# The same 1,706 steps in another order: the last 1,144 places of a written-out list, DeltaNet and a multiplicative FFN in one kernel

## The chip, the cores and the metric

One core of a Trainium2 chip runs the whole program. The metric is the device time of one execution in microseconds (us). TensorE is PE in the profile (its weight loads are PEld), VectorE is DVE, ScalarE is ACT, GpSimd is POOL, and SyncE is SP, which here issues all DMAs.

## The reference

A DeltaNet attention block over `q, k, v` of (4 batches, 8 heads, 768 tokens, 48) and `beta`, then a feed-forward block over its 3,072 tokens of 384 features, all float32.

```python
k_n = k / (norm(k) + 1e-6)
for t in range(S):
    y[t]  = q[t] @ state                       # state: 48 x 48 per batch and head
    v_old = state^T k_n[t]
    state = state + beta[t] * outer(k_n[t], v[t] - v_old)
x = y as (3072, 384)
out = ((x @ w1) * (x @ w2)) @ w3 @ w_out       # w1, w2: 384 x 1024; w3: 1024 x 1024; w_out: 1024 x 384
```

## The kernel before, in words

The recurrence is cut into 12 chunks of 64 tokens, two chunks to a pair (u = 0 to 5). Inside a chunk the recurrence is a triangular system. The kernel inverts its 32 x 32 blocks on DVE, and the rest is small matmuls on TensorE. The feed-forward part runs on the 512 tokens of a pair with w3 @ w_out folded into one weight (w34, 1024 x 384) at the start. From u = 1 on, the two products with w1 and w2 are made by a scheme with sums of operands that saves matmuls, and the product with w34 is made by a Strassen-like scheme for all u.

Each part is a Python generator. One `next` of it is a **step** and issues the instructions of one engine (a group of matmuls, one elementwise operation, a few DMAs). A string, `ORDER`, lists which part takes its next step. So the n-th mention of a name is always that part's step n (counted from 0), wherever it stands. After the list has been walked, `in_text_order` ties every instruction to the one before it on its engine: **each engine runs its own instructions in the list's order**, SP its DMAs too. Between engines only data and buffers set the order.

```python
    def step(name):
        other[:] = name[len(name.rstrip("'")):]     # a prime: the other engine
        ...
        next(running[name], None)

    for name in ORDER.split():
        step(name)
    in_text_order()
```

The names, with the lines of the profile:
- `p m` (L297), 2 steps: SP loads the keys (8 DMAs), then the queries of chunk m, from m = 4 on into the same buffer. `d m` (L390), 4: DVE transposes the two halves of the keys, then of the queries. `k`, `v` (L269, L280): SP loads more copies of keys and values.
- `s m` (L456, L462), twice: PE makes the scores, DVE scales a part (L468), ACT copies the rest (L480), POOL masks it (L482).
- `u m` (L522): SP writes blocks of the scores to DRAM. `V j`, for the two chunks of a pair: 0 loads them back (L533), 1 and 2 set up a PSUM buffer on ACT, **3 to 33 are 31 pairs of dependent DVE operations** (L564, L569), 34 and 35 copy out on ACT (L578), 36 writes to DRAM. From step 1 to 36 V holds one of the two large PSUM buffers (`ps_w`); the products of s, e, c and y then share the other one.
- `e m`: 0 loads the inverse's blocks on SP (L594, L601), 1 transposes on DVE (L622), 2 and 4 are PE products (L639), 3 and 5 are ACT's reads of them (L664, L684).
- `c m`: 0, 2 and 4 are PE products (L710), 1, 3 and 5 DVE's reads of them (L741: residual, L750: X, L772: the next state). Each product needs the read before it, product 2 also e's result.
- `y m` (L809): PE makes a chunk's outputs, ACT copies them (L828), SP completes them for a pair (L839).
- `n`, `g`, `N`: normalizers of the values and keys, on POOL, DVE and ACT.
- `G u`: POOL's sums of token blocks (L200). `m u0`, `m u1`: 47 steps each, in which PE adds a product into one of four PSUM banks (`ps_f`, L1140, two matmuls of 256 columns) and ACT (L1164, L1168) or DVE (L1166, L1171) reads it; step 30 (29 in `m u0`), 36 (34), 45 (44) and 46 multiply two results elementwise (L200).
- `S u`: POOL's sums of those results (L200), eight steps for u > 0. `oA u` to `oD u`: eight matmuls of 192 columns a step (L1222), A, B and C with two steps. `xA u` to `xD u`: ACT and DVE read those banks (L1252, L1257, L1259), SP stores the result (L1239). Banks come free for m of the next pair only by these reads. The last pair has `o5` and `x5`.
- `a`, `b` (L938): the two plain products of u = 0. `W`, `T`: POOL's sums of weights.

G, S, W and the elementwise products run on POOL; with a prime behind the name (`S4'`) on DVE:

```python
    def alone(out, x, y, op):
        (dve if other else pool).tensor_tensor(out=out, in0=x, in1=y, op=op)
```

PSUM banks and most buffers are handed out in turn at the step that first uses them (`in_turn`), so a list in another order also hands them out in another order.

Of the kernel before, what the change touches and what calls it, by code (L numbers as in the profile page):

```python
# [70 lines left out]
s6 G2 G2 m20 m20 m20 m20 m20 V3 m20 m20 m20 g4 V3 V3 V3 xC1 m20 m20 m20 d8 m20 m20 m20 m20 V3 V3 m20
d8 N3 m20 m20 m20 m20 m20 m20 m20 m20 m20' c6 m20 m20 m20 m20 m20 m21 g4 V3 e6 e6 m20 e6 m20 m20 m21
m21 e6 e6 m20 m20 g4 g4 m20 m20 g4 m21 m21 m21 e6 c6 c6 s8 m21 m21 m21 m21 N4 N4 s8 s8 m21 y6 m21
m21 m21 y6 c6 s8 p9 e7 e7 d9 d9 m21 m21 m21 m21 m21 m21 m21 c6 s8 e7 m21 s8 m21 m21 m21 p9 m21 e7 s8
d9 d9 m21 m21 m21 m21 m21' m21 s9 s9 s9 k10 s7 g5 s9 s9 n7 m21 m21 m21 s9 m21 m21' m21 m21 u8 e7 s9
c7 m21 m21 m21 c7 m21 u9 V4 S2' m21 m21 oA2 e7 m21' m21 S2 S2 g5 V4 S2 xA2 c7 oD2 V4 V4 V4 V4 c7 y7
V4 V4 V4 V4 V4 V4 p10 d10 V4 V4 y7 oB2 oA2 S2 s8 S2 S2 xB2 v8 y7 S2 d10 V4 V4 V4 V4 xA2 xA2 oB2 oC2
xB2 xD2 V4 V4 xC2 V4 V4 V4 V4 V4 V4 xC2 G3 G3 G3 m30 V4 m30 m30 xD2 m30 oC2 xC2 G3 G3 m30 m30 G3 G3
G3 G3 G3 m30 c7 m30 V4 V4 V4 V4 V4 m30 m30 m30 m30 m30 m30 m30 m30 m30 m30 m30 m30 V4 g5 n8 V4 V4 V4
v9 p10 k11 xC2 m30 m30 m30 G3' G3 m30 m30 m30 m30 m30 m30 m30 m30 m30 m30 m30 m30 c7 V4 e8 m30 m30  # L80
d10 m30 m30 m30 m30 m31 m30 m30 m31 m31 e8 e8 m30 e8 m31 c8 m31 e8 e9 g5 g5 n8 m30 m30 m31 m31 g5 g5
d10 g5 e8 n9 m30 n9 e9 c8 e9 c8 N4 m31 m31 m31 m31 m31 e9 m31 N5 m31 c8 y8 y8 N5 m31 m31 m31 p11 d11
# [13 lines left out]
m50 m50 m50 m50 m50 m51 m50 m50 m50 m50 m51 m51 m51 m51 m50 m50 m51 m50' m51 m51 m51 m51 m51 m51 m51
m51 m51 m51 m51 m51 m51 m51 m51 m51 m51 m51 m51 m51 m51 m51 m51 m51 m51 m51 m51 m51 m51 m51 S5' m51
m51 m51 m51 m51 m51 m51 m51 m51 m51 S5' o5 S5 m51' x5 S5 o5 o5 o5 o5 S5' S5 o5 x5 S5' x5 x5 S5' o5
x5 x5 x5 x5 x5 x5 x5 x5 x5 x5
# [1331 lines left out]
```

## Time and profile before

| | us |
|---|---|
| time, median of 3 runs (lowest, highest) | 545.23 (544.31, 548.61) |
| time of the profiled execution | 541.36 |
| its span, from the first to the last instruction | 539.7 |
| PE busy in it | 513.8 |
| DVE busy | 401.4 |
| POOL busy | 274.1 |
| ACT busy | 220.4 |

The profile names a wait by the engine that waits, its line, and what ended the wait. In the timeline the first number is the start in us from the span's start, the second the length, and `[0.85 <-DVE KQ L390]` says that the engine stood idle for 0.85 us until DVE's write of KQ at L390. A matmul in float32 is two instructions in the trace, so `x4` at L1140 is one step of m. The ends of matmuls are modelled; their starts are not, and times of steps are taken from start to start.

### The profile page before, as it was taken

The page shows a single profiled execution, that of the slowest core. Times are in us where ns is not written, and L with a number is a line of the kernel's source. Part 1 is how long each engine was busy: PE and PEld are TensorE (multiplying, and loading weights), DVE is VectorE, ACT ScalarE, POOL GpSimd, SP SyncE. Part 2 cuts the span into 40 slices and gives each one's busy share as a digit, 9 for nine tenths or more (in the row PEclk, how much of TensorE's full clock was granted, in tenths as well). Part 3 has the DMA queues.
Part 4 walks back from the last instruction along what each step waited for, and adds up shares of the span by engine and source line. Part 5 has one row for each costly group of instructions (what it writes and reads, how often), then busy time and mean ns, then how long its engine had stood idle before and what let it go on. Part 6 is the DMA issues. An engine that isn't in the chain of part 4 may idle for free.

```text
span 539.7 us, 19914 instructions
## 1 busy us (share of the span) xinstructions
PE 513.8 (95%) x8466; PEld 431.7 (80%) x8466; DVE 401.4 (74%) x880; ACT 220.4 (41%) x453; POOL 274.1 (51%) x296
## 2 busy tenths in 40 slices
PE   6779988999999999999999999999999999999997
PEld 3645557688888987789888889878799788997886
DVE  2789966898668997868997799887779855536562
ACT  3697567747534034432034433245321352312210
POOL 4585664244889996067832258361378402051150
PEclk8599998999999999999999999999999999999999
DMA  9969964869653354654454561733314220010001
GB/s 223 315 155 237 220 107 121 159 154 152 95 86 70 74 128 69 98 118 75 92 105 61 82 119 46 146 70 50 57 51 109 75 41 4 17 56 3 2 1 58
DMA packets 195544, 52.64 MB, mean 98 GB/s; under 512 B 182528, under 2 KB 189824, under 8 KB 195456
## 3 DMA queue, kind: packets, MB, share of 16 engines
q1 hardware_dynamic: 195456, 51.38, 46.3%
q8 instruction: 66, 1.08, 0.8%
q14 instruction: 22, 0.18, 0.1%
HBM read 41.25 MB, written 8.91 MB: 93 GB/s over the span
## 4 chain that ended last, share of the span: by engine, by line
PE 77%; DVE 6%; SPq 6%; DMA 4%; issue 3%; ACT 2%; POOL 1%; DVEq 0%; ACTq 0%; POOLq 0%
PE ps_f L1140 27%; PE ps_f L1222 20%; PE ps_f L938 8%; PE ps_w L710 6%; PE ps_f L918 5%; PE ps_w L809 4%; SPq L297 3%; PE ps_w L639 2%; PE ps_w L456 2%; PE ps_w L462 1%; DMA X<-in_q_dram 1%; DMA TT<-Vd 1%; SPq L269 1%; DVE KQ L390 1%; DMA perm<-in_q_dram 1%
## 5 line engine op out<-in xcount | busy, mean ns | idle before, releaser
L200 POOL TENSOR_TENSOR ab<-ab 128x512 f32<-128x512 f32 (+1 forms) x57 | 65.5, 1168 | 67.3 <-DVE ab L1171 33.7
L1222 PE MATMUL ps_f<-w,ab 128*128 128x192 f32 x376 | 65.1, 327 | 0.0
L1140 PE MATMUL ps_f<-xT,w1s 128*128 128x256 f32 x240 | 63.5, 388 | 0.1
L1140 PE MATMUL ps_f<-xT,w2s 128*128 128x256 f32 x240 | 61.6, 387 | 1.0 <-DVE x_room L1171 1.0
L1222 PEld LDWEIGHTS ps_f<-w,ab 128*128 128x128 f32 x376 | 61.9, 190 | 0.6
L1171 DVE TENSOR_TENSOR ab<-ab,ps_f 128x512 f32<-128x512 f32 x70 | 47.6, 683 | 16.7 <-PE ps_f L1140 15.0
L1140 PEld LDWEIGHTS ps_f<-xT,w1s 128*128 128x128 f32 x240 | 43.5, 189 | 9.8 <-ACT x_room L1168 2.0
L1140 PEld LDWEIGHTS ps_f<-xT,w2s 128*128 128x128 f32 x240 | 43.7, 189 | 8.6 <-DVE x_room L1171 1.5
L482 POOL TENSOR_TENSOR PT<-PT,smask 128x512 f32<-128x512 f32 x20 | 25.4, 1273 | 46.0 <-ACT PT L480 45.9
L1222 PE MATMUL ps_f<-room,ab 128*128 128x192 f32 x272 | 47.2, 329 | 0.8 <-DVE room L1252 0.8
L569 DVE TENSOR_TENSOR ps_w<-ps_w,tb 128x31 f32<-128x31 f32 (+15 forms) x124 | 43.3, 349 | 4.5
L564 DVE TENSOR_TENSOR tb<-ps_w,Ub 128x31 f32<-128x31 f32 (+15 forms) x124 | 41.9, 338 | 5.2 <-DMA Ub<-Ud 2.1
L918 PE MATMUL ps_f<-w2s,w3T 128*128 128x384 f32 x128 | 43.8, 492 | 1.7 <-POOL w2s L867 1.1
L1222 PEld LDWEIGHTS ps_f<-room,ab 128*128 128x128 f32 x272 | 44.2, 190 | 1.4 <-POOL xT L200 0.9
L828 ACT COPY xT<-ps_w 48x256 f32<-48x256 f32 x96 | 30.5, 365 | 33.6 <-PE ps_w L809 33.1
L200 POOL TENSOR_TENSOR xT<-xT 128x256 f32<-128x256 f32 x44 | 31.8, 738 | 21.0 <-DVE xT L200 15.2
L1140 PE MATMUL ps_f<-xT,room 128*128 128x256 f32 x160 | 39.9, 381 | 0.0
L918 PEld LDWEIGHTS ps_f<-w2s,w3T 128*128 128x128 f32 x128 | 23.4, 190 | 17.4 <-POOL w2s L867 2.4
L1171 DVE TENSOR_TENSOR x_room<-x_room,ps_f 128x512 f32<-128x512 f32 x40 | 27.2, 679 | 11.1 <-PE ps_f L1140 10.0
L1168 ACT COPY x_room<-ps_f 128x512 f32<-128x512 f32 x20 | 11.7, 585 | 55.9 <-PE ps_f L1140 44.2
L456 PE MATMUL ps_w<-KQ 48*64 48x128 f32 x384 | 28.6, 286 | 5.7 <-ACT KQ L204 1.8
L1140 PEld LDWEIGHTS ps_f<-xT,room 128*128 128x128 f32 x160 | 30.1, 190 | 4.1
(196 smaller groups left out, 1059.5 us busy)
## 6 DMA issues: line engine op xcount, KB each, us to landing
raw<-in_moe_w_dram SPq DMA_DIRECT2D x16, 512.0 KB, 5.5
ktok<-in_k_dram SPq DMA_DIRECT2D x48, 96.0 KB, 3.5
vtok<-in_v_dram SPq DMA_DIRECT2D x24, 192.0 KB, 4.3
raw<-in_moe_w_dram SPq DMA_DIRECT2D x24, 192.0 KB, 4.3
out_dram<-osb SPq DMA_DIRECT2D x46, 96.0 KB, 1.7
raw<-in_moe_w_out_dram SPq DMA_DIRECT2D x8, 384.0 KB, 4.2
perm<-in_k_dram SPq DMA_DIRECT2D x40, 64.0 KB, 3.3
perm<-in_q_dram SPq DMA_DIRECT2D x32, 64.0 KB, 2.7
```

The source lines that it names most:

```text
L200: (dve if other else pool).tensor_tensor(out=out, in0=x, in1=y, op=op)
L456: pe.matmul(ps[half(z), 0, n : n + 128], lhsT=x[:, 0, :], rhs=x.rearrange("p j t -> p (j t)"), start=True, stop=True,)
L482: pool.tensor_tensor(out=PT, in0=PT, in1=smask[:].unsqueeze(1).to_broadcast([P, H, C]), op=ALU.mult)
L564: dve.tensor_tensor(out=tv, in0=V[:, 0 : s + 1, s : s + 1].to_broadcast([P, s + 1, n]), in1=U[:, s, s + 1 : BS].unsqueeze(1).to_broadcast( ...
L569: dve.tensor_tensor(out=o, in0=o, in1=tv, op=ALU.subtract)
L710: pe.matmul(out(ps, r, h, z), lhsT=lhs(r, h, z), rhs=rhs(r, h, z), start=True, stop=True,)
L828: act.copy(out=xT[f, cc, p:NP:2, b : b + NR, :].rearrange("p a r t -> p r a t"), in_=pyv[f, z, b : b + NR],)
L918: pe.matmul(ps[:, 0:DM], lhsT=w3Ts[jc, kc // 4][:, kc % 4 * P : kc % 4 * P + P], rhs=wo[:, kc], start=(i == 0), stop=(i == KF - 1),)
L938: pe.matmul(ps[:].rearrange("p b c t -> p b (c t)"), lhsT=w[:, m, js], rhs=x[:, c0, m], start=(m == 0), stop=(m == KM - 1),)
L1140: pe.matmul(ps[:, n * g : n * g + n].rearrange("p (b c t) -> p b c t", b=HB, c=2), lhsT=product_weights(i, 2 * r + g), rhs=of[i], start=na ...
L1171: dve.tensor_tensor(out=t, in0=t, in1=cell(what[2]), op=op)
L1222: pe.matmul(ps[b][:, b, :], lhsT=block(u, HF * f + i, z)[:, P * b : P * b + P], rhs=ws_[w][:, i], start=first and i == 0 and (b == 0 or n ...
```

## The change

The first 562 steps stand as they were. The others stand in another order. No name is added or removed, but some primes sit at other mentions: 16 elementwise steps go from POOL to DVE and 14 from DVE to POOL. The lists are broken into lines at other places, so that the diff shows every line as changed. From it, the stretches around the places that are spoken of below (a stretch begins and ends in the middle of things; "..." is left out):

```diff
-u4 v4 b5 a05 W W n3 n4 e3 s5 b5 a04 W' W S0 u5 V2 e3 c2 N2 V2 c2 V2 a07 c3 b1 a05 c3 b1 V2 V2 c3 c3
-V2 a07 V2 V2 V2 V2 V2 oA0 V2 V2 y3 S0 S0' W W S0 S0 S0 n4 S0 xA0 oA0 oD0 W p6 S0 S0 S0 S0 y3 S0 S0
...
-m10 m10 m10 m10 g3 m10 m10 g3 m10 m10 m10 m10 m10 d6 g3 m10 W g3 g3 e4 g3 c4 G1 m10 m10 m10 m10 e4
-c4 m10 d6 p7 m10 m10 m10 m11 e4 e4 g3 g3 G1 m10 e5 m10 m11 m11 s4 e4 c4 c4 m10 m10 m10 m10' N3 m11
...
-m11' S1 oA1 S1 S1 m11 y5 oD1 y5 xA1 p8 oB1 g4 S1 V3 V3 V3 V3 V3 V3 V3 V3 V3 V3 V3 S1 oA1 S1 g4 V3 V3
-y5 G2 G2 V3 xB1 V3 c5 xA1 oB1 v6 c5 d8 V3 V3 oC1 xB1 V3 V3 xA1 xC1 k9 c6 xC1 m20 V3 d8 V3 V3 xD1 xD1
...
-m31 m31 m31 d11 p11 m31 m31 s10 s10 c8 m31 m31 c8 m31 m31 m31 s10 s9 s10 s10 c9 m31 d11 s10 m31 s10
-d11 c9 m31 m31 m31 u10 s11 s11 s11 s11 s11 m31 S3 m31 s11 m31 m31 m31' m31 m31 m31 e9 m31 m31 m31
-m31 m31 m31 S3 oA3 e9 s11 u11 V5 V5 c9 xA3 V5 c9 oD3 y9 y9 V5 V5 V5 V5 V5 V5 V5 V5 S3 m31 S3 s10 S3
-S3 V5 V5 oB3 xB3 V5 V5 oA3 y9 G4 G4 S3 S3 V5 V5 V5 V5 V5 oB3 xB3 V5 G4 G4 G4 G4 G4 oC3 xA3 xA3 xC3
...
+s4 s4 s4 s4 d5 s4 d5 a04 e3 s4 b7 b6 b4 b7 s5 s5
+s5 s5 s5 T s5 u4 v4 b5 a05 W W n3 n4 e3 s5 b5
+a04 W' a05 c2 e3 c2 W N2 a07 c3 c3 S0 b1 b1 a07 S0
+S0' c3 c3 S0 oA0 S0 S0 S0 S0 u5 V2 V2 V2 W xA0 y3
+y3 V2 V2 V2 V2 V2 V2 V2 V2 V2 V2 V2 V2 V2 V2 V2
+V2 k6 p6 oB0 xB0 W W oA0 W xA0 oD0 S0 c3 S0 y3 S0
+S0' S0 S0 S0 G1 G1 d6 V2 S0 V2 xA0 V2 G1 G1 G1 V2
+oB0 xB0 k7 G1 d6 G1 xD0 xD0 G1 G1 oC0 m10 xC0 xC0 m10 V2
...
+m10 m10 m10 m10 m10 m10 W m10 m10 m10 m10 m10 m10 d6 e4 e4
+c4 c4 m10 m10' m10 m10 m10 e4 p7 G1 m10 e4 e4 m10 m10 m11
...
+V3 xA1 m11 S1 S1 v7 S1 oD1 m11 y5 y5 y5 V3 V3 V3 V3
+V3 oB1 V3 N3 V3 V3 V3 V3 S1 S1 oA1 xB1 G2 V3 V3 oB1
+oC1 d8 V3 G2 xA1 S1 S1 xA1 V3 xB1 V3 xD1 V3 m20 m20 xC1
...
+p9 e7 e6 g4 m21 N4 c6 c6 N4 s8 s8 y6 y6 m21 m21 m21
...
+k10 g5 N4 e7 e7 s9 s9 s9 s9 s9 m21 m21 m21 s9 m21 m21
+s9 g5 m21 m21 m21 e7 S2 e7 c7 m21 c7 c7 m21 m21 m21 oA2
...
+m31 m31 m31 m31 m31 m31 m31 m31 s8 c8 y8 y8 m31 p11 d11 d11
+m31 m31 m31 m31 m31 m31 m31 m31 m31 m31 e9 c8 c8 s10 s10 s10
+s10 s10 s10 p11 d11 d11 s10 s10 m31 c9 c9 s11 s11 s11 s11 s11
+m31 m31 s11 m31 m31 m31 m31 m31 S3 m31 e9 N5 m31 m31 m31 u10
+u11 s11 e9 m31 m31 oA3 c9 m31 oD3 S3 V5 V5 c9 s9 V5 V5
+V5 V5 V5 V5 V5 V5 V5 V5 y9 S3 S3 S3 S3 oB3 xA3 V5
+v10 y9 y9 xB3 V5 V5 V5 V5 m31 oA3 V5 xA3 S3 xA3 oB3 xB3
+V5 V5 S3 V5 n10 n10 oC3 xC3 c9 V5 V5 V5 xD3 G4 G4 G4
...
+m51 m51' m51 m51 m51 m51 m51 m51 m51 m51 m51' m51 xC4 o5 o5 x5
+o5 S5 S5 S5' S5' S5 S5' S5 x5 x5 S5' o5 o5 x5 o5 x5
+x5 x5 x5 x5 x5 o5 x5 x5 x5 x5
```

More of the change, by code (lines that the diff above doesn't have):

```diff
@@ L71 @@
[L71 to L80, printed above, removed]
@@ L96 @@
[L96 to L99, printed above, removed]
+warm+3 P11 beta P2 P0 P11 P11 P11 P2 beta P3 k0 K0 P0 beta P0
+P0 K0' K0 P6 P6 k1 K1 zd zd zd P2 g0 P2 P9 P3 q0
+K0 K0 g0 g0 g0 g0 g0 P6 P9 g0 g0 K1 P9 P3 K1 P16
+K1 q1 Q0 P10 Q0' N0 K1' P6 P16 P16 P3 Q0 Q0 Q0 P12 P13
@@ new lines @@
+V5 V5 V5 V5 V5 V5 xD3 G4 G4 m40 m40 c9 m40 m40 G4 m40
+G4' m40 m40 m40 m40 m40 m40 m40 m40 m40 m40 m40 m40 m40' m40 m40
+m40 m40 m40 m41 c10 G4 m40 e10 e10 e10 m40 m40 m40 m40 m40 m41
+m41 m41 m41 m41 m41 e10 c10 m40 m41 m41 m41 e10 m41 m41 m41 m41
+e10 c10 m41 m41 m41 m41 m41 e11 v11 n11 e11 c10 e11 n11 c10 c10
+m41 m41 m41 m41 m41 m41 m41 m41 m41 m41 m41 m41' m41 e11 e11 e11
+c11 m41 m41 m41 m41 m41' m41 m41 m41 S4 y10 c11 c11 c11 m41 m41
+m41 m41 m41 s11 y10 oA4 xA4 y11 m41' oD4 S4' y11 y11 S4' S4 oB4
```

104 lines of the change are left out of this document (68 added, 36 removed).

## The prediction

> **What bounds the kernel now.** I read the totals of the page first, then busy time by stages, then TensorE's own waits, and last the instructions around its gaps.
>
> ```profile
> span 539.7 us, 19914 instructions
> PE 513.8 (95%) x8466; PEld 431.7 (80%) x8466; DVE 401.4 (74%) x880; ACT 220.4 (41%) x453; POOL 274.1 (51%) x296
> ...
> 160.00:200.00 40.00, 39.87 (x623) 36.04 (x622) 34.21 (x84) 11.46 (x26) 38.81 (x48) 1.00 0.43 86
> ...
> 247.00:281.00 34.00, 33.09 (x298) 29.89 (x291) 31.48 (x78) 8.99 (x22) 22.70 (x26) 1.00 0.44 91
> ...
> 392.00:430.00 38.00, 37.88 (x432) 33.70 (x431) 31.94 (x80) 10.12 (x25) 25.34 (x28) 1.00 0.31 78
> ...
> PE ps_f L1140 <- DVE x_room L1171: 1.0, 2, 0.8
> PE ps_w L456 <- ACT PT L480: 0.9, 1, 0.9
> PE ps_f L1222 <- DVE room L1252: 0.8, 1, 0.8
> PE ps_w L456 <- DVE KQ L390: 0.8, 1, 0.8
> ```
>
> The three stage rows give, after the length, the busy time of PE, PEld, DVE, ACT and POOL, and the granted clock. The last four are all of PE's waits from 140 us on: 3.5 us. The first changed step is c2's third product, at about 161 us. So in the part that the change touches TensorE is busy all the time at full clock, with VectorE over 80% busy beside it where an inverse (V) runs. A list with the same matmuls can win little more than PE's gaps. Measured from start to start they are a little longer:
>
> ```profile
> 225.41 0.76 PE L639 MATMUL ps_w<-T,U 33*33 33x32 f32 x64
> 227.01 0.82 PE L456 MATMUL ps_w<-KQ 48*64 48x128 f32 x3 [0.85 <-DVE KQ L390]
> ...
> 255.01 1.14 PE L710 MATMUL ps_w<-X,ktok 64*64 64x48 f32 x64
> 257.00 1.21 PE L1222 MATMUL ps_f<-room,ab 128*128 128x192 f32 x6 [0.85 <-DVE room L1252]
> ...
> 381.10 1.03 PE L1140 MATMUL ps_f<-xT,w1s 128*128 128x256 f32 x4
> 383.01 0.33 PE L456 MATMUL ps_w<-KQ 48*64 48x128 f32 x2 [0.89 <-ACT PT L480]
> ...
> 385.03 1.13 PE L1140 MATMUL ps_f<-xT,w1s 128*128 128x256 f32 x4
> ...
> 387.96 0.76 PE L639 MATMUL ps_w<-T,T 33*33 33x32 f32 x64
> 388.95 1.13 PE L1140 MATMUL ps_f<-xT,w2s 128*128 128x256 f32 x4 [0.23 <-DVE x_room L1171]
> ...
> 514.66 1.13 PE L1140 MATMUL ps_f<-xT,w1s 128*128 128x256 f32 x4
> 515.83 0.69 DVE L1171 TENSOR_TENSOR x_room<-x_room,ps_f 128x512 f32<-128x512 f32 x1 [0.23 <-PE ps_f L1140]
> 516.58 1.13 PE L1140 MATMUL ps_f<-xT,w2s 128*128 128x256 f32 x4 [0.78 <-DVE x_room L1171]
> ...
> 286.92 0.69 PE ps_w L639 x50
> 287.61 1.92 PE ps_f L1140 x8
> 289.54 1.08 PE ps_w L710 x64
> ...
> 293.49 1.49 PE ps_w L809 x96
> 295.09 0.67 PE ps_w L809 x32
> 295.76 1.92 PE ps_f L1140 x8
> ...
> 315.30 2.60 PE ps_f L1222 x16
> ```
>
> The last rows, from the chain that ended last, price the steps: an e product 0.69 us, two m products 1.92 (0.96 each), a c product 1.08, a y step 2.27 (293.49 to 295.76), an o product 2.60; two s products lie between 383.01 and 385.03, 1.0 each. By these the five gaps are 1.60 - 0.69 = 0.9; 1.99 - 1.08 = 0.9; 1.91 - 0.96 = 0.95; 0.99 - 0.69 = 0.3; 1.92 - 0.96 = 0.96: **4.0 us**, 0.7% of the span. That is the largest gain there is, bar small change.
>
> **The change part by part.** All 1,144 steps that stand elsewhere keep their instructions and DMAs, so matmuls, bytes and DMA issues add and remove nothing. What changes is each engine's own order, including SP's queue of DMAs, and the engine of 30 elementwise steps (16 go from POOL to DVE, 14 the other way). For each PE step I asked what it waits for and how much PE work the new list puts between producer and consumer.
>
> Gone. (1) The gap at 257.00 waits for xB1's first sum, which stood behind 14 pairs of V3 on DVE, with one o product (2.6 us) between V3's first pair and it in the list. Now 13 pairs stand before it, and oD1, y5, oB1 and oA1's second product lie between (about 10 us). V3 starts earlier against PE: -0.9. (2) At 227.01 the scores s7 wait for d7's transposes. p7's loads keep their place on SP behind e4's and e5's, but V2 and d6, which free DVE and p7's buffer, end sooner; d7's last transposes still stand only a few steps ahead of s7: I take 0.2 left (0 to 0.9): -0.7. (3) At 383.01 the wait is s11's, for d11.
>
> ```profile
> 374.01 1.18 SPq L297
> ...
> 377.89 2.84 DMA perm<-in_q_dram
> ```
>
> p11's query load takes 6.7 us from issue (374.01) to landing (380.73), so d11 cannot end before 382. In the new list c8's third product and both s10 stand after y8 and a run of m31, later than the load can be issued, so -0.95; what comes in its place is priced below. (4) At 516.58 nothing changes: step 40 of m51 directly follows step 38 in both lists, with DVE's read of step 38's bank between them (1.17 to its start, 0.69 long): 0.96 stays. The same pair of m31 has e9's product between in both: 0.3 stays. Removed: 0.9 + 0.7 + 0.95 = **2.55**.
>
> Added. These rows give the round trips:
>
> ```profile
> 206.46 0.76 PE L639 MATMUL ps_w<-T,U 33*33 33x32 f32 x64
> 207.45 1.16 ACT L664 COPY T<-ps_w 32x512 f32<-32x512 f32 x2
> ...
> 431.18 1.15 PE L710 MATMUL ps_w<-S,KQ 48*64 48x48 f32 x64
> 432.45 0.95 DVE L741 TENSOR_TENSOR vtok<-vtok,ps_w 128x768 f32<-128x768 f32 x1 [0.45 <-issue]
> ```
>
> From an e product's start to the end of ACT's copies is 207.45 + 1.16 - 206.46 = 2.15, and from a c product's start to the end of DVE's read 432.45 + 0.95 - 431.18 = 2.2; with the matmul's own start about 2.3 for c.
> - `e4 m10 e4`: 0.69 + 0.96 = 1.65 of 2.1: **0.4** (two m products stood there before).
> - `c7 m21 c7`: 1.08 + 0.96 = 2.0 of 2.3: **0.3**.
> - `c6 s8 y6`: y6 needs X from c6, with one s product of 1.0 between: 0.2; and before c6, ACT does a copy of m21 ahead of e6's last: 0.3. Together **0.5**.
> - `e7 s9 s9`: s9's second product takes e7's PSUM buffer: 1.7 of 2.1: **0.4**.
> - `c8 s10 s10`: the second takes c8's buffer: 2.1 of 2.3, and then s11 stands behind d11, now placed after s10's second sum on DVE: 0.3 + 0.5 = **0.8**.
> - POOL before oA3's second product: m31 step 45, S3 steps 1 to 5, s9's mask and m31 step 46 stand in a row, and oA3 reads step 46's result.
>
> ```profile
> L200 POOL TENSOR_TENSOR ab<-ab x57: 716/1269/1725, 166.9 to 523.4; 128x512 f32<-128x512 f32 x42, 128x256 f32<-128x256 f32 x15
> L200 DVE TENSOR_TENSOR ab<-ab x19: 415/691/1533, 174.1 to 531.3; 128x512 f32<-128x512 f32 x18, 128x256 f32<-128x256 f32 x1
> L200 DVE TENSOR_TENSOR ab<-x_room,late x5: 687/692/1758, 215.9 to 520.4; 128x512 f32<-128x512 f32 x5
> ...
> 395.32 0.19 DVE L564 TENSOR_TENSOR tb<-ps_w,Ub 128x31 f32<-128x31 f32 x1 [0.54 <-DMA Ub<-Ud]
> ...
> 409.21 0.42 DVE L564 TENSOR_TENSOR tb<-ps_w,Ub 128x252 f32<-128x252 f32 x1
> 409.66 0.43 DVE L569 TENSOR_TENSOR ps_w<-ps_w,tb 128x252 f32<-128x252 f32 x1
> ```
>
> Eight times 1.27 is 10.2 us. The row starts when m31's last bank has been read, some 1.7 us into oA3's first product, and the second comes 11.15 us after that product's start (oA3, c9, oD3, y9, oB3: three times 2.6, 1.08, 2.27), its second block an eighth of 2.6 later: 11.9 against 11.5, **0.5**. The same row of POOL work before oA2's second: **0.2**.
> - xD3 stands behind 21 pairs of V5 where it was 18. A pair is 0.9 us there (409.21 to 410.09), so 2.7 later on DVE, while V5's first pair now stands ahead of y9 and not behind it, 2.27 of PE work earlier: **0.4** for m40's second step, which takes that bank.
>
> Added: 0.4 + 0.3 + 0.5 + 0.4 + 0.8 + 0.7 + 0.4 = **3.5**. Each could be 0 (the reader runs a little sooner) or twice as long (one more instruction ahead of it): 0 to 7.0.
>
> The 30 swapped steps: alone, one takes 0.69 on DVE and 1.27 on POOL, and most lie under PE work. The rows show up to 1.76 on DVE and 1.73 on POOL for the same shape. The one pair on the path is m51's steps 45 and 46, which change places: C11 now comes from DVE at the moment C12 starts on POOL, before o5's second product. I take nothing, as both have an o product of 2.6 in front; between -0.2 (DVE is faster alone) and 1.07 (1.758 - 0.691). The Trainium skill, page "SBUF — State Buffer", section "SBUF: two separate sides", says that the second of a GpSimd operation and a DVE operation with two SBUF inputs is blocked until the first ends. The longest times agree with such blocking. By that rule the sum would be about 0.4 higher, an estimate.
>
> SP: k7 now stands before xD0's store and waits for c3's third product, and p11 behind e9's loads; the queue is empty again before V2's and d11's needs, so 0 (to 1.0 if a load lands late). The tail after o5's last product is the same order of reads and stores: 0.
>
> **Sum**: -2.55 + 3.5 = +0.95. The profiled execution took 541.36 (span 539.7 and 1.7 around it), so 542.3. The median shown, 545.23, lies 3.87 above it: 546.2.
>
> **Rivals.** (a) *Only the gaps go*: the new close spots have slack that I don't see, since I added up least distances. Then 545.23 - 2.55 = 542.7; with all 4.0 gone 541.2. For it: POOL and ACT idle half the time. Against: e4, c7 and c8 are plain arithmetic. Faster by over 1% (539.8) needs 5.4 us, more than PE waits for; only smaller hand-over gaps everywhere could give it. (b) *VectorE is late in the V bursts, slower*: V2, V4 and V5 start by their list place only if their block loads have landed. The 395.32 row waited 0.54 for that DMA. If the loads and not the list set the start, the bank reads behind V come late by what I counted as gained, about 2 to 2.7 us in each of three bursts; from 0.4 us of lateness on, PE stops there. That adds about 6: 552.2. For it: DVE at 84 to 93% in those stages; against: the blocks come from s products that also stand earlier. (c) *The list is different and the chip doesn't care*: PE takes the same total to 0.3 us: 545.2.
>
> **How the numbers follow.** About 1% is what a measurement of this kernel can tell from no change (runs lie from 544.31 to 548.61). Forecast (541.8 to 549.4) with (c): 0.63 + 0.07; (a) 0.13, of which 0.05 beyond 1%; (b) 0.17. Same: 0.70 + 0.08 = 0.78. The range must hold 8 in 10: from 541.8, in (a), to 551.0, with both ends of the added 0 to 7.0 and part of (b).
>
> **What would show it.** Right: PE waits of about 4 us after 160 us, none at xB1, one each in front of oA3's second product, between the two e4 products, at s10 or s11, and at m51's step 40. Wrong: a single PE wait over 2 us, most likely on `DVE room L1252` or `osb` in a V burst, or a clock below 1.00 after 160 us.

## The result: slower by 1.1%, with new stops of TensorE and half clock behind some of them

The changed kernel takes **550.94 us** (median of 17 runs, 547.31 to 555.71) where the kernel before, run beside it, takes 545.49 (17 runs, 538.99 to 548.61). The ratio is 1.0112, 95% interval 1.0086 to 1.0138: 5.45 us slower, where I had forecast 0.95. The profiled execution of that comparison was the slowest of the 17 (555.71), so I mostly read a second profile of the same kernel, of an execution of 548.12 us. In all profiles from here on the line numbers are those of before plus 47: s is L503 and L509, e L686, c L757, y L856, m L1187, d L437, p L344.

From the page and from TensorE's waits from 150 us on, second profile of the changed kernel:

```profile
span 546.4 us, 19910 instructions
PE 521.8 (95%) x8466; PEld 437.7 (80%) x8466; DVE 403.6 (74%) x882; ACT 220.6 (40%) x453; POOL 274.5 (50%) x294
...
PEclk8569998999999999999999999999999998999999
```

```profile
PE ps_w L757 <- issue: 1.7, 2, 1.5
PE ps_w L503 <- DVE KQ L437: 1.3, 2, 1.1
PE ps_w L856 <- issue: 1.0, 1, 1.0
PE ps_f L1187 <- DVE x_room L1218: 0.8, 1, 0.8
PE ps_w L503 <- ACT T L711: 0.4, 1, 0.4
PE ps_f L1269 <- POOL ab L247: 0.2, 1, 0.2
```

The matmuls are the same 8,466, but PE is now busy for 521.8 us instead of 513.8: some of it at half clock, most of that in the unchanged first 160 us, and one slice behind it (the 8 in the row of the clock). A new releaser is on top with 2.7 us together: `issue`, which means that PE waited for nothing the profile shows. It had no row at all among before's waits in this stretch. The waits that the prediction took away are indeed gone: no wait at xB1 (L1269 `<- DVE room`).

The three costly places, PE's timeline in the same profile:

```profile
293.56 0.42 PE L856 MATMUL ps_w<-KQ,S 48*48 48x64 f32 x10
295.02 0.49 PE L856 MATMUL ps_w<-KQ,S 48*48 48x64 f32 x20 [1.05 <-issue]
...
297.16 1.99 PE L1187 MATMUL ps_f<-xT,w2s 128*128 128x256 f32 x8
...
383.76 1.15 PE L757 MATMUL ps_w<-S,KQ 48*64 48x48 f32 x64
386.06 0.82 PE L503 MATMUL ps_w<-KQ 48*64 48x128 f32 x3 [1.15 <-DVE KQ L437]
...
447.86 0.96 PE L757 MATMUL ps_w<-X,ktok 64*48 64x48 f32 x49
450.30 0.39 PE L757 MATMUL ps_w<-X,ktok 64*64 64x48 f32 x13 [1.49 <-issue]
450.62 3.49 PE L1187 MATMUL ps_f<-xT,spare 128*128 128x256 f32 x8
453.90 1.26 PE L1187 MATMUL ps_f<-xT,w1s 128*128 128x256 f32 x4
```

y6 stops in the middle of its own matmuls, after 10 of 128, and c10's third product after about 50 of 64: the matmuls on both sides of the stop read the same operands, so it is not data that is missing. s11 stops for d11. And behind c10 two m products take 3.28 us instead of 1.92 (453.90 - 450.62): half clock. Start to start, over the plain times of the prediction, the places cost (in us; s11's 1.2 is its wait, 0.5 its first product, slow behind it)

| | predicted | second profile |
|---|---|---|
| xB1 | -0.9 | -0.9 |
| s7 (before: 1.5) | -0.7 | 0.8 left: -0.7 |
| s11 for d11 (before: 0.95) | -0.95 + 0.5 | 1.2 + 0.5: +0.75 |
| s8 and y6 | +0.5 | 0.4 + 1.3: +1.7 |
| c10's third product | 0 | +1.7, and 1.4 at half clock |
| e4; c7; s9; s10 | 0.4; 0.3; 0.4; 0.3 | 0.3; 0.4; 0.65; 0.4 |
| POOL rows at oA2, oA3; xD3 | 0.7; 0.4 | 0.2; 0 |
| kept: m51 step 40 | 0.96 | 0.96 |

Those that were priced from a round trip came out within 0.3. s7's row holds for this profile alone: the first profile has the same 0.85 of waiting there as before, so nothing gained. The rows that changed add up to +5.9. From the first changed product to the end the second profile takes 5.2 us more than the one of before (161.9 to 543.9 against 160.8 to 537.6), close to the 5.45 of the medians.

### The profile page after: what moved, and what is told of

Read it like the earlier page. It is cut to its first block, busy times and chain, and to the rows that moved or that the text cites. A ratio compares the mean times of both kernels' runs of the same rounds, so it can differ in the third digit from the quotient of the medians.

```text
span 553.2 us, 19910 instructions
## 1 busy us (share of the span) xinstructions
PE 521.3 (94%) x8466; PEld 436.5 (79%) x8466; DVE 403.0 (73%) x882; ACT 220.5 (40%) x453; POOL 274.5 (50%) x294
## 4 chain that ended last, share of the span: by engine, by line
PE 68%; DVE 12%; DMA 7%; SPq 6%; issue 3%; ACT 2%; POOL 1%; DVEq 0%; ACTq 0%
PE ps_f L1187 29%; PE ps_f L1269 16%; PE ps_f L985 7%; PE ps_w L757 5%; PE ps_w L856 4%; SPq L344 3%; DMA raw<-in_moe_w_dram 2%; DVE KQ L437 2%; PE ps_w L686 2%; DVE ps_w L605 1%; DVE tb L600 1%; DVE tb L611 1%; PE ps_f L965 1%; SPq L899 1%; PE ps_w L503 1%
## 5 line engine op out<-in xcount | busy, mean ns | idle before, releaser
L1269 PE MATMUL ps_f<-w,ab 128*128 128x192 f32 x376 | 65.3, 327 | 0.1
L1187 PE MATMUL ps_f<-xT,w1s 128*128 128x256 f32 x240 | 65.2, 395 | 0.1
L1187 PE MATMUL ps_f<-xT,w2s 128*128 128x256 f32 x240 | 61.9, 391 | 1.6 <-DVE x_room L1218 0.8
L1269 PEld LDWEIGHTS ps_f<-w,ab 128*128 128x128 f32 x376 | 61.7, 190 | 1.0 <-DVE osb L1299 0.5
L1187 PEld LDWEIGHTS ps_f<-xT,w1s 128*128 128x128 f32 x240 | 44.1, 194 | 10.7 <-ACT x_room L1215 1.9
L1187 PEld LDWEIGHTS ps_f<-xT,w2s 128*128 128x128 f32 x240 | 44.6, 192 | 9.7 <-DVE x_room L1218 1.4
L1269 PE MATMUL ps_f<-room,ab 128*128 128x192 f32 x272 | 47.7, 329 | 0.0
L1269 PEld LDWEIGHTS ps_f<-room,ab 128*128 128x128 f32 x272 | 44.2, 190 | 0.7
L247 POOL TENSOR_TENSOR xT<-xT 128x256 f32<-128x256 f32 x41 | 29.2, 728 | 26.5 <-DVE xT L247 16.7
L1187 PE MATMUL ps_f<-xT,room 128*128 128x256 f32 x160 | 39.7, 381 | 0.1
L503 PE MATMUL ps_w<-KQ 48*64 48x128 f32 x384 | 30.7, 293 | 7.0 <-DVE KQ L437 2.3
L437 DVE STREAM_TRANSPOSE KQ<-perm 128x512 f32<-128x512 f32 x36 | 24.6, 698 | 14.0 <-PE ps_w L856 4.4
L1187 PEld LDWEIGHTS ps_f<-xT,room 128*128 128x128 f32 x160 | 30.1, 190 | 4.5 <-DVE ab L1218 0.5
```

The source lines that it names most:

```text
L437: dve.transpose(out=KQ[:, bs, :, i, :].rearrange("p b a t -> p (b a) t"), in_=src[:, bs].rearrange("p b a x d -> p (b a) (x d)"),)
L503: pe.matmul(ps[half(z), 0, n : n + 128], lhsT=x[:, 0, :], rhs=x.rearrange("p j t -> p (j t)"), start=True, stop=True,)
L1187: pe.matmul(ps[:, n * g : n * g + n].rearrange("p (b c t) -> p b c t", b=HB, c=2), lhsT=product_weights(i, 2 * r + g), rhs=of[i], start=na ...
L1269: pe.matmul(ps[b][:, b, :], lhsT=block(u, HF * f + i, z)[:, P * b : P * b + P], rhs=ws_[w][:, i], start=first and i == 0 and (b == 0 or n ...
```

## Theory and rivals

**A**: stops of 1 to 2 us at named places, for missing instructions (y6, c10) or for d11 (s11), and a lower clock behind some of them. **B**: VectorE or POOL late for PSUM banks. **C**: the 30 steps that swapped engines. **D**: many small waits everywhere.

## First experiments: spread, bring forward, fill

The kernel again:

> The changed kernel unchanged, for a second profile beside the three below. Theory A (TensorE stands 1.5 us at y6, at s11 and behind c10's third product, and two of these stops are followed by 3.4 us at half clock, which costs more than the stop): the stops at y6 and c10 again show `issue` as the releaser, the one at s11 `DVE KQ L437`, and a half-clock window behind at least one of them; time 551, ratio to before 1.010. Rival B (VectorE or POOL late, the 30 swapped steps): waits on `osb`, `room` or `ab` between 560 and 1 us each in another place, clock 1.00. Rival D (many waits under 0.5 us): no single stop over 1 us that comes again.

Measured 548.25 us, ratio 1.0084 (1.0044 to 1.0123). The two `issue` stops and the one at s11 come again, each in the same place; half clock follows c10's here. For A.

```diff
-... c6 c6 N4 s8 s8 y6 y6 m21 m21 m21 m21 m21
+... c6 c6 N4 s8 s8 m21 m21 m21 y6 y6 m21 m21
-... e11 c10 e11 n11 c10 c10 m41 m41 m41 m41
+... e11 c10 e11 n11 m41 m41 m41 c10 c10 m41
```

> The changed kernel with y6 put three m21 steps later and c10's third product three m41 steps later, so that large products lie between them and the small ones before (s8, and e11). Theory A with loading of TensorE's instructions as the cause of these two stops: both `issue` stops go, with them the half clock behind y6; faster than the changed kernel by 3.2 + 1.7 = 4.9 of the profiled excess, at least 1.5 + 1.5 = 3.0. If the stops are waits for data (X from c6, S) the gain is the waits alone, under 1. Rival B: no change. Rival D: under 0.5.

549.54, ratio 1.0116 (1.0058 to 1.0175): **not faster**. In its profile c10 has no stop, and y6 has none, but PE stops 0.8 us for `issue` at an m21 right behind y6: the shortage had moved. And s11's stop was followed by 6.8 us at half clock, which in this profile takes back what c10 gave.

```diff
-... m31 p11 d11 d11 (10 m31) e9 c8 c8 s10 s10 s10 s10 s10 s10 p11 d11 d11 s10 s10
+... m31 p11 d11 d11 p11 (10 m31) d11 d11 e9 c8 c8 s10 s10 s10 s10 s10 s10 s10 s10
```

> The changed kernel with p11's query load put right behind d11's first two transposes and d11's last two ahead of e9's product, all else the same. Theory A: the wait of 1.4 us at s11 goes, and the half clock behind it (about 3.7 us in the profile): faster than the changed kernel by 3 to 5 us. If the half clock has another cause than the stop: faster by 1.4 at most and the half-clock window stays near 392. Rivals B and D: 0 to 1.4.

552.48, ratio 1.0201 (1.0143 to 1.0260): slower by 1% more. My edit was wrong, and its timeline says how:

```profile
382.52 1.30 DVE L437 STREAM_TRANSPOSE KQ<-perm 128x512 f32<-128x512 f32 x2 [3.35 <-DMA perm<-in_q_dram]
...
384.72 0.33 PE L503 MATMUL ps_w<-KQ 48*64 48x128 f32 x2 [4.26 <-DVE S L819]
```

The transposes stand earlier on DVE, but the queries land no earlier. DVE waits for them 3.35 us with c8's read of its bank behind it, and s10, which takes that bank, waits 4.26.

```diff
-... N4 s8 s8 y6 y6        -... c9 c9 s11 s11
+... N4 s8+2 s8 y6 y6      +... c9 c9 s11+2 s11
```

("+2" makes the step issue two idle products of 128 x 512 first.)

> The changed kernel with work added: two idle products of 128 x 512 (0.9 us each, written to the bank that the step then overwrites) ahead of s8's first product and two ahead of s11's. Nothing else is changed. Theory A: they cover the wait at s11, give the loading of instructions time before y6, and keep TensorE's clock full there; 3.6 us of work added, up to 3.2 + 5.2 taken away, so the kernel is not slower than the changed one and perhaps 2 to 4 us faster. Rivals B and D, or a half clock with another cause: the work is hidden only under the wait at s11 (1.4), so slower by 2.2 us.

545.31, ratio 1.0054 (1.0021 to 1.0087): **3.8 us of added work (1.91 start to start at each place), and 2.9 us less by the medians than the kernel without it, run beside it.** The two intervals overlap, so a gain is likely but not certain; the loss of 2.2 us that B and D ask for is not there. Its waits from 150 us on, the top ones:

```profile
PE ps_w L686 <- DVE wt L417: 1.2, 1, 1.2
PE ps_f L1187 <- DVE x_room L1218: 0.8, 1, 0.8
PE ps_w L503 <- ACT PT L527: 0.7, 1, 0.7
PE ps_w L757 <- issue: 0.7, 3, 0.3
```

The wait for d11 is under the added work, y6 has no `issue` wait any more, and from 160 us to the tail no half clock follows anything. Not all of the gain is the cover: c10's stop, which I hadn't touched, is 0.5 instead of 1.7 here. The work at the two places costs about what it hides (3.8 against 1.7 + 1.7), so the rest of the gain is c10's and that of half clock that doesn't come. B and D don't explain this.

## Second: later, spread everywhere, the reverse, the engines back

```diff
-... s10 p11 d11 d11 s10 s10 m31 c9 c9 s11 s11 s11 s11 s11 m31 m31 s11 m31 m31
+... s10 p11 s10 s10 m31 c9 c9 d11 d11 m31 m31 m31 m31 s11 s11 s11 s11 s11 s11
```

> The changed kernel with s11 three steps of m31 later (six list places, its steps 0 to 5) and d11's last two transposes behind c9's first read, so that nothing waits for p11's query load. Theory A: the wait at s11 (1.2 us in the second profile of the changed kernel) goes, and with it the half clock that follows it in some runs (about 1.7 us more, in 2 of 3 profiles): 1.2 to 3 us faster than the changed kernel, ratio to before about 1.005. If the load cannot be hidden, the wait stands elsewhere (in front of m31's banks or c9) and the time does not move. Rivals B and D: at most 1.2.

551.71, ratio 1.0145 (1.0086 to 1.0205). The wait went where the second case said:

```profile
PE ps_f L1187 <- DVE ab L1213: 1.8, 1, 1.8
```

DVE stands at d11 with m31's read behind it. All close spots at once (the edits of the second and fifth kernel, and one to three m products put between the other pairs):

```diff
+... e4 p7 G1 m10 m10 e4 e4 ... s8 s8 m21 m21 m21 y6 y6 m21 m21 n7 s8 s8 d9 d9 m21 m21 m21 m21 m21 c6 c6 s8
+... s9 s9 s9 s9 m21 s9 ... c7 m21 m21 c7 c7 ... s10 m31 s10 ... d11 d11 m31 m31 m31 m31 s11 ... m41 m41 m41 c10 c10
```

> The changed kernel with every close spot spread by one to three large products: e4's two products, s8 and y6, c6's third product, s9's two, c7's first two, s10's two, s11 and d11, and c10's third product. 30 swapped steps and all else stay as in the changed kernel. Theory A (dense small products and short dependencies make the stops, the stops lower the clock): the second profile of the changed kernel has 7.5 us over the plain sum of its TensorE steps from 150 us on, of which 1.7 at s8 and y6, 3.1 at c10, 1.7 at s11, 0.65 at s9, 0.4 at s10, 0.4 at c7 and 0.3 at e4: 8.2 with small gains elsewhere; without them about 543 where the changed kernel takes 550 and before 545: ratio to before 0.997 (0.992 to 1.002). Rival B or the engine swaps: still 1.005 or more.

548.67, ratio 1.0078 (1.0041 to 1.0115): a miss. s11's wait again sits at m31's bank (2.0), y6's 1.1 us behind it, and a new stop of 0.9 at e4 is followed by half clock.

The reverse, in the list of before:

```diff
-... c6 c6 s8 m21 m21 m21 m21 N4 N4 s8 s8 m21 y6 m21 m21
+... c6 c6 s8 y6 m21 m21 m21 m21 N4 N4 s8 s8 m21 m21 m21
-... m41 e11 e11 e11 c10 m41 m41 m41 m41 m41 m41 c10 m41 m41 c10 e11
+... m41 c10 m41 m41 m41 m41 m41 e11 c10 e11 c10 e11 m41 m41 m41 e11
```

> The kernel before with two groups of small products put together as the changed kernel has them: y6's first step right behind s8's first product, and c10's third product right behind e11's first. Nothing else is changed. Theory A: `issue` stops at y6 or behind it (1 to 1.5 us) and at c10 (1.5), with half clock behind one of them or both: 2.5 to 6 us slower than before, ratio 1.005 to 1.011. If the stops of the changed kernel come from something else in its list (buffers, late engines): within 0.5 us of before.

544.12, ratio 1.0002 (0.9964 to 1.0039): a miss, and the most useful one. y6 stops as in the changed kernel (0.7 for `issue`, 1.3 start to start with s8), but **c10 behind e11 does not stop at all**, and no half clock follows. Being close together isn't enough.

```diff
-S0' S0 S0 S0 G1 ... m10 m10' m10 m10 ... m11 S1' c5      (30 steps in all)
+S0 S0 S0 S0 G1 ... m10 m10 m10 m10 ... m11 S1 c5
```

> The changed kernel's order with the 30 elementwise steps back on the engines that the kernel before gives them. Theory A: these steps play no part, ratio to before 1.010, the same stops at y6, s11 and c10. Rival C (the swapped steps cost the time, by being slower on POOL or by keeping DVE from its reads): 2 to 5 us faster than the changed kernel, ratio 1.000 to 1.006.

556.20, ratio 1.0200 (1.0138 to 1.0262), 1% over the kernel with the swaps: C falls, with the sign turned round. A had given the swaps no part (1.010) and missed too. The old engines don't suit the new order, and here B's wait appears:

```profile
PE ps_f L1187 <- DVE osb L1299: 4.5, 1, 4.5
```

## Third: which stretch of the list

The two lists have nearly the same steps ahead of some common places, so stretches can be exchanged.

```diff
-places 562 to 1705 in the changed kernel's order
+places 562 to 984 in the changed kernel's order, all that is left in the order of before
```

> The changed kernel's list for its first 985 places (to the end of e6's first product, about 285 us), and from there all remaining steps in the order of the kernel before. Theory A' (the loss lies in places that can be named: s8 and y6, s9, s10 and s11, c10, all behind 285 us; the part ahead of it gains xB1's 0.9 and loses 0.3 at e4): ratio to before 0.999 (0.996 to 1.002). Rival (a change spread over the whole list, each part a little slower): ratio 1.003 to 1.006.

```diff
-places 562 to 1705 in the order of before
+the same, but from e6's first product to m31's first ones (places 988 to 1256) the changed kernel's order
```

> The kernel before, with the changed kernel's order only from e6's first product to m31's first product after it (285 to 360 us). Theory A': by the times from cut to cut in two profiles of the changed kernel against the one of before this stretch is 2.3 us longer in one (1.4 at y6, 0.6 at s9, 0.3 at c7) and 6.1 in the other: ratio 1.004 to 1.008. Rival (the loss is at s11 and c10 alone): 1.000 to 1.002.

```diff
-places 562 to 1705 in the order of before
+the same, but from m31's first products to e11's third (places 1259 to 1519) the changed kernel's order
```

> The kernel before, with the changed kernel's order only from 360 to 455 us (e9, s10, d11, s11, V5, c10, e11). Theory A': the wait for d11 at s11, the instruction stop at c10 and half clock behind one or both: 3.2 to 4.5 us longer by the times from cut to cut, ratio 1.005 to 1.009. If c10's stop depends on where the blocks of 256 instructions begin, and these lie otherwise here, only s11 is left: 1.002 to 1.004.

| changed order in | ratio to before | 95% interval |
|---|---|---|
| 160 to 285 us | 0.9997 | 0.9960 to 1.0033 |
| 285 to 360 us | 1.0064 | 1.0027 to 1.0101 |
| 360 to 455 us | 1.0066 | 1.0033 to 1.0099 |
| all (17 runs) | 1.0112 | 1.0086 to 1.0138 |

The parts add up (1.27% against 1.12); the last stretch, behind 455 us, was not run alone. The first stretch, with most of what I had priced as gains, costs and gains nothing that can be measured; the loss lies in the stretches of y6, s9 and c7, and of s11 and c10. A loss spread evenly over the whole list is ruled out.

```diff
 (as the first of these three)
-... e5 e5 s7 s7 s7 s7 m11 s7 s7     -... u10 s11 s11 s11 s11 s11 m31 S3 m31 s11 m31 m31
+... e5 e5 m11 m11 s7 s7 s7 s7 m11 m11 m11 s7     +... u10 m31 S3 m31 m31 m31 s11 s11 s11 s11 s11 s11
```

> The first of these four kernels, with two products of m11 moved ahead of s7's first and one ahead of its second, and two of m31 ahead of s11: it gives the waits for d7 and d11, 1.6 and 1.0 us in the profile of before, other work to lie under. Theory A': 2.6 us faster than that one, 3 us faster than before: ratio 0.994 (0.990 to 0.998). If the two loads cannot be hidden, the wait stands elsewhere and the ratio is that of the first.

548.21, ratio 1.0081 (1.0041 to 1.0120): a miss. s7's wait is gone, but s11 later puts 2.0 us in front of m31's bank and 2.1 behind e9.

## Fourth: what makes s11 wait

The chain to s11, DVE, SP and PE of before (old numbers: X is L750, y L809, d L390, p L297), then of the changed kernel:

```profile
363.68 5.03 SPq L297 DMA_DIRECT2D perm<-in_k_dram  x8
364.28 1.27 PE L710 MATMUL ps_w<-vtok,TT 64*64 64x48 f32 x64
365.48 1.13 PE L1140 MATMUL ps_f<-xT,room 128*128 128x256 f32 x4
366.45 1.89 PE L1140 MATMUL ps_f<-xT,w2s 128*128 128x256 f32 x8
368.27 0.67 PE L809 MATMUL ps_w<-KQ,S 48*48 48x64 f32 x32
...
372.32 1.30 DVE L390 STREAM_TRANSPOSE KQ<-perm 128x512 f32<-128x512 f32 x2 [0.54 <-DMA perm<-in_k_dram]
373.66 4.72 SPq L297 DMA_DIRECT2D perm<-in_q_dram  x8
```

```profile
365.84 5.04 SPq L344 DMA_DIRECT2D perm<-in_k_dram  x8
366.55 1.27 PE L757 MATMUL ps_w<-vtok,TT 64*64 64x48 f32 x64
...
371.32 0.95 DVE L797 TENSOR_TENSOR X<-ps_w,wt 128x768 f32<-128x768 f32 x1
...
373.13 0.66 PE L856 MATMUL ps_w<-KQ,S 48*48 48x64 f32 x32
...
375.53 1.30 DVE L437 STREAM_TRANSPOSE KQ<-perm 128x512 f32<-128x512 f32 x2 [2.67 <-PE ps_w L856]
...
376.86 5.05 SPq L344 DMA_DIRECT2D perm<-in_q_dram  x8
```

In the changed list d11 waits for y8 (it takes y8's key buffer), and the query load for d11. y8 stands six m31 products behind c8's second product (366.55) where before has three: 6.6 us from start to start instead of 4.0, in which PE never stops. From the start of the key load it is 11.0 us to the query load instead of 10.0. In before d11 waits for the keys themselves. N5's chain of small DVE operations now stands ahead of c8's second read too, so that X is written only at 372.27; but y8's product with X starts at 373.61, so X is not what held y8 here. The next edit moves both.

```diff
-... c8 m31 g5 g5 g5 N5 N5 m30 m31 m31 m31 m31 m31 m31 ... s8 c8 y8 y8 m31 p11 d11 d11
+... c8 m31 g5 g5 g5 m30 m31 c8 N5 N5 m31 m31 m31 m31 s8 y8 y8 m31 m31 p11 d11 d11
```

> The changed kernel with c8's second read put ahead of N5 on DVE, as in the kernel before, and y8, p11's key load and d11's first two transposes some six steps of m31 earlier. In the changed kernel X comes at 371.3 behind N5's 3.4 us of small DVE operations (364.0 in one profile of a list with the old order there), y8 at 373.1 and p11's query load at 376.9 (372.4). If that lateness is what makes s11 wait: the load is issued 3 to 4 us earlier against TensorE, the wait at s11 (1.2 and 0.5) goes without coming up at m31's banks, and the time falls by 1.7 to 3.4 (where a half clock followed): ratio to before 1.005 to 1.008. If the load's own length or SP's queue sets it: no change, 1.010.

The same edit in the list with the changed order from 360 to 455 us alone:

> The kernel before with the changed kernel's order only from 360 to 455 us, and in it the same edit as in the one above (c8's second read ahead of N5, y8 and d11's first half earlier). That stretch alone cost 0.66% in the run before this. If the wait for d11 is the stretch's loss: ratio 1.000 to 1.003. If something else in the stretch costs it (V5, oA3, c10): 1.005 or more.

And with y6 and c10 spread:

> The changed kernel with the same edit, and y6 three products of m21 and c10's third product three of m41 later. The named stops (s8 and y6 1.7, c10 1.7 and sometimes half clock, s11 1.7 and sometimes half clock) are 5 us in one profile of the changed kernel, so by them the ratio is 1.000 to 1.003. If what is lost at one stop comes back at the next one (the loads and instruction blocks come when they come): 1.006 or more.

547.94, ratio 1.0099 (1.0064 to 1.0134); 546.37, 1.0073 (1.0038 to 1.0107); 548.32, 1.0123 (1.0073 to 1.0173). None is faster. s11 has no wait left in all three, but each has a new one of 2.1 us at m31's bank, and the third kernel's ACT and DVE show what makes it:

```profile
PE ps_f L1187 <- DVE late L1218: 2.1, 1, 2.1
...
379.07 2.57 ACT L875 COPY xT<-ps_w 48x256 f32<-48x256 f32 x8 [5.56 <-PE ps_w L856]
381.65 0.58 ACT L1215 COPY late<-ps_f 128x512 f32<-128x512 f32 x1
...
382.27 0.69 DVE L1218 TENSOR_TENSOR late<-late,ps_f 128x512 f32<-128x512 f32 x1 [1.90 <-ACT late L1215]
```

With y8 its eight copies on ACT have come forward, and ACT's read for m31 stands behind them; DVE's, which frees the bank, adds to what ACT has written. The same copies stand there in the other two, where DVE waits 0.34 and 0.87 for ACT; in the first of them it had waited 1.66 for the keys before. So these three show that the wait for d11 can be taken away, and that my edit put ACT's queue in its place; a list that moves y8 and keeps ACT's read ahead of its copies was not run. In the list that ran at the time of before I moved only s7, and d11 with the query load:

```diff
-... c8 y8 y8 N5 m31 m31 m31 p11 d11 m31 m31 m31 d11 p11      (and s7 as above)
+... c8 y8 y8 N5 m31 p11 d11 d11 p11 m31 m31 m31 m31 m31
```

> The list whose first 985 places are the changed kernel's and the rest in the order of before (it ran at the time of before), with two products of m11 ahead of s7's first and one ahead of its second, and d11's first two transposes and p11's query load right behind y8. No step of s11 is moved. The waits at s7 (0.3 to 1.0, and 0.65) go, and the query load is issued 1.5 to 2 us earlier so that s11's 0.7 goes too: 1.6 to 2.4 us faster than before, ratio 0.996 (0.993 to 0.999). If moving these only moves the waits: 1.000 or more.

542.84, ratio 1.0006 (0.9970 to 1.0043): no gain, with 1.8 us at m31's bank in place of s7's and s11's waits. Here it is the keys: DVE waits 1.22 at d11 for them to land, with the read of the bank right behind it.

## Fifth: cover the wait, and the best list of these runs

```diff
-... c9 c9 s11 s11 s11      (in the list with the changed order from 360 to 455 us)
+... c9 c9 s11+2 s11 s11
```

> The list that has the changed kernel's order only from 360 to 455 us, with two idle products of 128 x 512 (0.9 us each, into the bank that s11 then overwrites) ahead of s11's first product: 1.8 us of work put into a wait of 1.3 + 0.5. If a stop of this length costs itself and in some runs 3.4 us at half clock behind it (half clock behind s11 in 3 of 5 lists that have the stop, 1.8 us on average), the added work is hidden and the half clock gone: ratio 1.003 (1.000 to 1.005) where the list without it has 1.0066. If the stop costs itself alone: 1.0066 as before or 0.1% more.

546.10, ratio 1.0027 (0.9992 to 1.0062) where the list without the fills had 1.0066 (1.0033 to 1.0099): as A expects, though the intervals overlap and the plain medians hardly differ.

```diff
-... e5 e5 s7 s7 s7 s7 m11 s7 s7 s6      (in the list of the first stretch)
+... e5 e5 m11 m11 s7 s7 s7 s7 m11 m11 m11 s7 s7 s6
```

> The list whose first 985 places are the changed kernel's and the rest in the order of before, with two products of m11 ahead of s7's first and one ahead of its second, and nothing else moved. In the two lists with this edit s7's waits were gone (0.4 left of 0.9 to 1.6) and no other wait came up there. 0.5 to 1.2 us faster than without, with fewer half clocks behind s7 (in 2 of 5 lists): ratio to before 0.997 (0.993 to 1.001). If it changes nothing that can be measured: 1.000.

542.03, ratio 0.9960 (0.9927 to 0.9993): the only interval of these kernels that lies below 1. The order is that of the changed kernel up to 285 us, that of before behind it, and s7 with work put ahead of it. It is one measurement of 18, and the interval overlaps that of the same list without the edit (0.9960 to 1.0033). Its profile doesn't show the gain, DVE and PE around s7:

```profile
226.82 1.30 DVE L437 STREAM_TRANSPOSE KQ<-perm 128x512 f32<-128x512 f32 x2 [0.72 <-DMA perm<-in_q_dram]
228.05 0.65 DVE L1218 TENSOR_TENSOR x_room<-x_room,ps_f 128x512 f32<-128x512 f32 x1
...
228.75 1.13 PE L1187 MATMUL ps_f<-xT,w1s 128*128 128x256 f32 x4 [0.46 <-DVE x_room L1218]
```

s7 itself loses only 0.1 now, but the two m11 products ahead of it take 2.65 instead of 1.92: DVE still stands at d7 for the queries, with m11's read of a bank behind it, and the second product waits for that bank. The list without the edit loses 0.8 at s7 in its profile, so nothing is won there. In the other two lists with this edit the products take 2.43 and 2.46, and without it s7 loses 0.8 to 1.5 in eleven profiles of the changed order: the edit hides part of the wait and moves the rest.

## Why the prediction was wrong, and where it was right

- **Sum of gaps, right for what waits for data.** xB1, e4, c7, s9 and m51 came out within 0.3 of their terms; the POOL rows and xD3 cost less than priced (0.2 of 1.1). That s7's -0.7 came out too is luck: the place loses 1.5 in before, as its first product is 0.6 slow behind the wait, which the 0.9 of the prediction leaves out, and in the first profile of the changed kernel it loses 1.5 again.
- **Step (3) of what goes, s11, failed.** It said that the query load could be issued early enough because c8's third product and both s10 stand after y8. SP's place of a load says nothing when the load waits for a buffer: this one waits for d11's first transposes, and these for y8, which the changed list has three m31 products later. From y8's start it is 12.9 us by that chain to s11's (373.13 to 386.06), and the list puts 11.7 us of TensorE's work there. The forecast for s11 was -0.95 + 0.5, and +0.75 came. What I let pass, the wait behind the order of an in-order engine, is what foiled my edits around d11 and y8 as well (on DVE, and on ACT in three).
- **The term for `c6 s8 y6` was mis-sized**, 0.5 against 1.7, since I priced only data; and **c10 was missing from the sum** (1.7, with half clock 3.1). Both are `issue` stops, at a border between two blocks of TensorE's instructions (below). Before's trace had them in the unchanged part, 3.1 us at L710 with 1.94 at 80.24, and I didn't read ahead of 140 us.
- **The clock was left out of the sum.** I named a clock under 1.00 as a sign of being wrong, but gave no stop a price beyond itself. In the windows of the first profile the stop at y6 costs 3.2 start to start with 1.5 of waiting, and s11's is followed by 6.8 us at half clock; in the second c10's costs 3.1.
- The time, 550.94, lies just inside the stated range, whose upper end was 551.0. That is luck: the end was made of waits for data twice as long as priced and part of rival (b), not of instruction stops and half clock.
- Rival (b), VectorE late in V bursts, was not it: from 150 us on the second profile has no wait on `osb` or `room`, the first one of 0.7 on `osb`. The swapped steps at 0 were on the safe side: back on their old engines they cost 1% more.
- Open: the profiles of the two bad stretches alone show 2.5 and 1.5 us of the 3.5 and 3.6 by the ratios. Half clock differs from execution to execution and would fill the rest, but that is argued, not shown. What c10 alone costs in the whole list was not timed.

## What to carry to other kernels

Where an engine is busy to 95%, price a reordering by what each new neighbour waits for, follow a moved load back to what frees its buffer, and follow each wait on an in-order engine to what stands behind it. In these lists a step moved ahead of its data only moved the wait, and independent work put in front of the reader hid it where that work needed nothing of the engine that waits (the idle products), and only in part where it did (m11). A stop of about 1.5 us on TensorE can cost twice itself, and small matmuls in a row can outrun their instructions; large products put between them took c10's stop away here, and moved y6's to the product behind it.

## What the runs showed of the hardware

**Half clock goes by a grid.** From the clock's records of all 20 profiles here: half clock starts only at multiples of 3.41 us, and from 60 us on it lasts one such window or two. Behind a window at full clock in which PE stood idle for 1.48 us or more (23 windows from 60 us on) half clock followed 22 times; at 1.3 to 1.48 us 3 times of 11; at 0.8 to 1.3 us 3 times of 47. Two windows and their followers in the first profile of the changed kernel, the last in one of before (columns: window, length, PE, PEld, DVE, ACT, POOL busy, clock, DMA):

```profile
293.60:297.00 3.40, 1.76 (x84) 1.48 (x80) 2.93 (x12) 0.07 (x1) 0.00 (x0) 0.99 0.61 74
297.00:300.40 3.40, 3.30 (x114) 2.95 (x103) 1.64 (x6) 0.07 (x1) 0.00 (x0) 0.50 0.11 13
389.10:392.50 3.40, 1.89 (x95) 1.55 (x90) 2.01 (x3) 0.07 (x1) 1.38 (x2) 1.00 0.47 78
392.50:395.90 3.40, 3.40 (x75) 3.15 (x69) 2.11 (x4) 0.59 (x1) 1.10 (x1) 0.51 0.02 5
```

```profile
77.80:81.20 3.40, 1.46 (x47) 1.11 (x43) 0.66 (x1) 0.52 (x2) 1.16 (x1) 1.00 0.57 76
81.20:84.60 3.40, 3.38 (x112) 3.16 (x108) 2.56 (x5) 2.13 (x4) 0.00 (x0) 0.50 0.79 172
```

The grid lies elsewhere in each execution, so a stop of 1.5 us falls into one window or is cut in two, and costs 1.5 or, with 1.7 lost at half clock, 3.2 us. c10's stop is 1.49 long in both profiles of the changed kernel: in the second it falls into one window (447.54 to 450.95) and half clock follows, in the first a border (457.39) leaves 1.31 of it in one window and none does. The Trainium skill, page "TensorE: Matmul & The Clock Gate", section "Part 1: The HAM clock gate", gives the same grid of 3413 ns, but half clock after at least one idle window. By that, from 60 us on, only the stop of 4.5 us at `osb` in the kernel with the old engines, which leaves one window wholly idle, would lower the clock; the traces show that a window idle for less than half is enough.

**Instructions can be late.** The traces have 66 or 67 packets of 16,384 bytes on the instruction queue for 16,932 matmuls and weight loads, some 256 to a packet, and one never starts less than 3.2 us after the last. The stops lie at one place of this count: number all of PE's records in a trace (matmuls, weight loads and its few other instructions) from 0 by their starts, and each of the 42 `issue` stops of over 0.5 us from 60 us on in the 20 profiles comes at a number that is 193 or 194 more than a multiple of 256. PE's other waits are spread over about 50 places of the count. Each `issue` stop of over 0.5 us at y6 and c10 ends 2.2 to 2.9 us after a packet's start (second profile: 292.82 to 295.02, 447.90 to 450.30). Where c10 did not stop, its packet had started 1.9 or more ahead of it; where it did, from 0.9 ahead to 0.2 behind, but for the list with fills (1.4 ahead, 0.5 of stop). So it goes by where the blocks of 256 begin, and the same neighbours stop in one list and not in another. The Trainium skill, page "Runtime: NRT & Kernel Launch", section "Instruction fetch mechanics", has blocks of 256 instructions too, and calls the cost of crossing one mostly hidden; in dense small matmuls it isn't, with stops of up to 1.6 us at y6 and up to 2.6 in the unchanged part.
